# A 16 KiB copy from HBM to HBM as the first transfer of a streaming kernel

## The chip, the cores and the metric

The kernel runs on one core of one Trainium2 chip. The metric is the device time of one execution in microseconds, as a median over runs. A profile is one more execution, recorded by the hardware profiler; its span runs from the first to the last recorded instruction and is a little shorter than the device time.

## What is computed

The reference adds a scaled tensor to another. All tensors are bf16; `x` and `fx` have 512 x 32 x 640 elements (20.97 MB each), `alpha` is one number.

```python
B, S, D = 512, 32, 640
def reference(x, fx, alpha):
    return x + alpha * fx
```

So 41.94 MB have to be read from HBM and 20.97 MB written.

## The kernel before

Each tensor is seen as 128 rows (partitions) of 81,920 elements, that is 80 pieces of K = 1024 elements, or 160 KiB a row. `xv`, `fxv` and `ov` are these views of `x`, `fx` and the output. The tables `X` and `FX` cut the 80 pieces into tiles: x in three tiles of 32, 32 and 16 pieces, fx in five of 16, 16, 19, 16 and 13. The pool `wide` has two buffers for x tiles, `fs` two for fx tiles. The result is written over the x tile in SBUF (on-chip memory), and the x tile is what gets stored.

The order is written out by hand in `PLAN`, one step a line, and kept as it stands:

- `x i` (`load_x`, L73, its DMA at L77) loads x tile i. `X_CUTS` cuts tile 0 in two transfers: 4 pieces (1 MiB), then 28 pieces (7 MiB).
- `f j` (`load_f`, L82, DMA at L85) loads fx tile j.
- `a` (`alpha_to_lanes`, L109) loads alpha (DMA at L111), spreads it over 128 partitions with one matmul by a row of ones (L115), and copies the result from PSUM to `a_f` (L117).
- `c j i` (`compute`, L88, instruction at L92) does x + alpha * fx on VectorE (DVE) where fx tile j and x tile i overlap, one `scalar_tensor_tensor` instruction.
- `s i` (`store`, L102, DMA at L104) stores x tile i to the output.

All 13 DMA transfers are issued by SyncE (SP) on one queue, in the order of the plan: x tile 0 (two pieces), alpha, fx 0, fx 1, x 1, fx 2, store 0, fx 3, x 2, fx 4, store 1, store 2. The first six need no buffer that was used before and wait for nothing; the later ones wait for DVE or an earlier transfer to free a buffer or finish a tile. SP handles its instructions in order, so a waiting one holds up all that stand behind it.

At the end, `rest` (L126) makes SP wait for everything in `done` but the last store before the program's own closing wait for that store. `done` is the list to which each step appends its instruction.

The change adds one line between `store` and `lanes`, ahead of the loop over `PLAN`, and one constant.

Of the kernel before, what the change touches and what calls it, by code (L numbers as in the profile page):

```python
# [2 lines left out]

# [4 lines left out]

ACT = mybir.ActivationFunctionType
ALU = mybir.AluOpType  # L10
F32 = mybir.dt.float32
BF16 = mybir.dt.bfloat16

K = 1024
P = 128


X = [(0, 32), (32, 64), (64, 80)]
FX = [(0, 16), (16, 32), (32, 51), (51, 67), (67, 80)]

X_CUTS = {0: (4,)}
PLAN = """
x 0
a
f 0
f 1
x 1
c 0 0
f 2
c 1 0  # L30
s 0
f 3
x 2
c 2 1
f 4
c 3 1
c 3 2
s 1
c 4 2
s 2  # L40
"""


@with_exitstack
def kernel(
    ctx: ExitStack,
    tc: tile.TileContext,
    x: bass.AP,
    fx: bass.AP,
    alpha: bass.AP,  # L50
    out: bass.AP,
):

    nc = tc.nc
    xv = x.flatten_outer_dims().rearrange("(p n) d -> p (n d)", p=P)
    fxv = fx.flatten_outer_dims().rearrange("(p n) d -> p (n d)", p=P)  # L60
    ov = out.flatten_outer_dims().rearrange("(p n) d -> p (n d)", p=P)
    assert xv.shape[1] == X[-1][1] * K == FX[-1][1] * K

    consts = ctx.enter_context(tc.tile_pool(name="consts", bufs=1))
    psum = ctx.enter_context(tc.tile_pool(name="psum", bufs=1, space=bass.MemoryType.PSUM))
    wide = ctx.enter_context(tc.tile_pool(name="wide", bufs=2))
    fs = ctx.enter_context(tc.tile_pool(name="fs", bufs=2))
    ctx.enter_context(tc.manual_schedule())

    xt, ft = {}, {}  # L70
    done = []

    def load_x(i):  # L73
        a, b = X[i]
        xt[i] = wide.tile([P, max(e - s for s, e in X) * K], x.dtype, tag="x", name="x_t")
        for c, d in pairwise((a, *X_CUTS.get(i, ()), b)):
            r = nc.sync.dma_start(  # L77
                out=xt[i][:, (c - a) * K : (d - a) * K], in_=xv[:, c * K : d * K]
            )
            done.append(r)  # L80

    def load_f(j):  # L82
        a, b = FX[j]
        ft[j] = fs.tile([P, max(e - s for s, e in FX) * K], fx.dtype, tag="f", name="f_t")
        r = nc.sync.dma_start(out=ft[j][:, : (b - a) * K], in_=fxv[:, a * K : b * K])  # L85
        done.append(r)

    def compute(j, i):  # L88
        (fa, fb), (xa, xb) = FX[j], X[i]
        a, b = max(fa, xa), min(fb, xb)  # L90
        piece = xt[i][:, (a - xa) * K : (b - xa) * K]
        r = nc.vector.scalar_tensor_tensor(  # L92
            out=piece,
            in0=ft[j][:, (a - fa) * K : (b - fa) * K],
            scalar=lanes["a_f"][:],
            in1=piece,
            op0=ALU.mult,
            op1=ALU.add,
        )
        done.append(r)  # L100

    def store(i):  # L102
        a, b = X[i]
        r = nc.sync.dma_start(out=ov[:, a * K : b * K], in_=xt[i][:, : (b - a) * K])  # L104
        done.append(r)

    lanes = {}

    def alpha_to_lanes():  # L109
        a_1 = consts.tile([1, 1], alpha.dtype, name="a_1")  # L110
        done.append(nc.sync.dma_start(out=a_1[:], in_=alpha[None, :]))  # L111
        ones = consts.tile([1, P], alpha.dtype, name="ones")
        nc.vector.memset(ones[:], 1.0)  # L113
        a_ps = psum.tile([P, 1], F32, name="a_ps")
        done.append(nc.tensor.matmul(a_ps[:], ones[:], a_1[:], start=True, stop=True))  # L115
        lanes["a_f"] = consts.tile([P, 1], F32, name="a_f")
        nc.vector.tensor_copy(out=lanes["a_f"][:], in_=a_ps[:])  # L117

    does = {"x": load_x, "f": load_f, "c": compute, "s": store, "a": alpha_to_lanes}
    for step in PLAN.split("\n"):  # L120
        if step:
            what, *of = step.split()
            does[what](*map(int, of))


    rest = nc.sync.nop(nofuse=True)  # L126
    info = mybir.DependencyInfo(mybir.DependencyClass.Sync, mybir.DependencyReason.DATA)
    for i in done[:-1]:
        tc.add_manual_dep(rest.ins, i.ins.name, info, reason="all but the last store")


# [1 line left out]
_INS = ['x', 'fx', 'alpha']  # L133
_OUTS = [((512, 32, 640), 'bfloat16')]


# [23 lines left out]
```

## Time and profile before

| what | value |
|---|---|
| device time, median of 3 runs | 152.08 us (152.06 to 152.09) |
| span of the profiled execution | 150.2 us |
| DVE busy | 86.8 us, in 8 instructions |
| DMA | 1,730 packets, 62.92 MB, 419 GB/s over the span |
| HBM read, written | 41.94 MB, 20.97 MB |
| first piece of x (1024 KB), issue to landing | 4.8 us |
| second piece of x (7168 KB), issue to landing | 21.3 us |
| SP's first store and next load issued at | 66.78 and 67.19 us |

How to read the profile: an engine's busy time counts its compute instructions; issuing a DMA is not counted as busy. The row of the DMA queue tells how many packets went through it, their megabytes, and the time that they took as a share of what 16 DMA engines have in the span. The chain of waits follows the work that ended last back through what released it; the timeline lists instructions by their start; a table of windows gives, for each stretch of time, the busy time of each engine, the granted TensorE clock, and the DMA's share and rate. SPq is SP's queue of DMA issues. A window books a packet to the stretch in which it starts, so that short windows with long packets swing around the true rate.

The profiled execution's own time is its span of 150.2 us and what lies around the span; the difference to the median of the runs is 1.88 us.

### The profile page before, as it was taken

How to read it: one execution, taken by the hardware profiler on the slowest of the kernel's cores; microseconds unless marked ns; L12 is line 12 of the kernel's file. 1: busy time of each engine (PE TensorE's matmuls, PEld its weight loads, DVE VectorE, ACT ScalarE, POOL GpSimd, SP SyncE). 2: the span in 40 equal slices, each digit the busy share in tenths (PEclk: the TensorE clock that was granted, in tenths of full speed). 3: DMA queues.
4: the chain of work that ended last, by engine and by line, in shares of the span. 5: the costliest groups of instructions: out<-in, count | busy, mean ns of one | idle time of the engine just before them, and what ended most of it. 6: DMA issues, size and time to landing. Idle time of an engine off the chain costs nothing.

```text
span 150.2 us, 78 instructions
## 1 busy us (share of the span) xinstructions
PE 0.2 (0%) x1; PEld 0.1 (0%) x1; DVE 86.8 (58%) x8; POOL 0.2 (0%) x4
## 2 busy tenths in 40 slices
PE   0000000000000000000000000000000000000000
PEld 0000000000000000000000000000000000000000
DVE  0000000049999999970399999106999999980000
POOL 0000000000000000000000000000000000000000
DMA  5997989999969696999696999999999969696994
GB/s 179 589 428 305 489 384 419 436 454 471 576 297 559 279 559 279 497 394 435 279 559 279 559 401 410 445 419 419 419 393 454 620 279 559 279 559 297 454 463 183
DMA packets 1730, 62.92 MB, mean 419 GB/s; under 512 B 194, under 2 KB 194, under 8 KB 194
## 3 DMA queue, kind: packets, MB, share of 16 engines
q1 hardware_dynamic: 1730, 62.92, 98.1%
HBM read 41.94 MB, written 20.97 MB: 419 GB/s over the span
## 4 chain that ended last, share of the span: by engine, by line
DMA 54%; DVE 35%; SPq 1%; issue 0%; DVEq 0%
DMA f_t<-in_fx_dram 54%; DVE x_t L92 35%; SPq L77 1%; SPq L111 0%; DVEq L92 0%
## 5 line engine op out<-in xcount | busy, mean ns | idle before, releaser
L92 DVE SCALAR_TENSOR_TENSOR x_t<-f_t,a_f,x_t 128x16384 bf16<-128x16384 bf16 (+3 forms) x6 | 86.5, 14438 | 25.5 <-DMA f_t<-in_fx_dram 25.5
L117 DVE COPY a_f<-a_ps 128x1 f32<-128x1 f32 x1 | 0.2, 159 | 21.5 <-PE a_ps L115 21.5
L113 DVE MEMSET ones<- 1x128 bf16 x1 | 0.2, 165 | 0.8 <-PEq L144 0.8
L115 PE MATMUL a_ps<-a,ones 1*128 1x1 bf16 x1 | 0.2, 158 | 22.2 <-DMA a<-in_alpha_dram 22.2
L144 POOL MEMSET const-bfloat16-1.0<- 128x1 bf16 x1 | 0.1, 103 | 0.0
L144 POOL MEMSET const-uint8-127<- 128x1 uint8 x1 | 0.1, 103 | 0.0
L115 PEld LDWEIGHTS <-ones 1*128 1x128 bf16 x1 | 0.1, 100 | 1.0 <-DVE ones L113 1.0
L144 POOL MEMSET const-float32-1.0<- 128x1 f32 x1 | 0.1, 100 | 0.0
L144 POOL MEMSET const-float32-0.0<- 128x1 f32 x1 | 0.1, 99 | 0.2 <-issue 0.2
## 6 DMA issues: line engine op xcount, KB each, us to landing
f_t<-in_fx_dram SPq DMA_DIRECT2D x3, 4096.0 KB, 35.6
x_t<-in_x_dram SPq DMA_DIRECT2D x1, 7168.0 KB, 21.3
f_t<-in_fx_dram SPq DMA_DIRECT2D x1, 4864.0 KB, 24.1
x_t<-in_x_dram SPq DMA_DIRECT2D x1, 4096.0 KB, 19.2
out_dram<-x_t SPq DMA_DIRECT2D x1, 4096.0 KB, 14.9
f_t<-in_fx_dram SPq DMA_DIRECT2D x1, 3328.0 KB
x_t<-in_x_dram SPq DMA_DIRECT2D x1, 1024.0 KB, 4.8
out_dram<-x_t SPq DMA_DIRECT2D x2, 24.7
```

The lines of the kernel that those rows point to most:

```text
L77: r = nc.sync.dma_start(out=xt[i][:, (c - a) * K : (d - a) * K], in_=xv[:, c * K : d * K])
L92: r = nc.vector.scalar_tensor_tensor(out=piece, in0=ft[j][:, (a - fa) * K : (b - fa) * K], scalar=lanes["a_f"][:], in1=piece, op0=ALU.mult ...
L113: nc.vector.memset(ones[:], 1.0)
L115: done.append(nc.tensor.matmul(a_ps[:], ones[:], a_1[:], start=True, stop=True))
L117: nc.vector.tensor_copy(out=lanes["a_f"][:], in_=a_ps[:])
L144: nc = _bacc.Bacc("TRN2", target_bir_lowering=False, num_devices=1)
```

## The change

One more transfer is issued on SP's queue before the plan's first step. It copies the first 512 elements (1 KiB) of each of the first 16 rows of the view of x to the same place in the output, directly from HBM to HBM, 16 KiB in all. The first 512 elements of these rows belong to x tile 0, so store 0 writes the same bytes of the output again later, with the result. The transfer is appended to `done`. Nothing else differs; on all other engines the instructions stand as before, and on SP the others follow in their old order. In the changed file, lines from the new constant on move down by one, and those behind the new transfer by three.

```diff
 FX = [(0, 16), (16, 32), (32, 51), (51, 67), (67, 80)]
 
+HEAD = 16
 X_CUTS = {0: (4,)}
...
         r = nc.sync.dma_start(out=ov[:, a * K : b * K], in_=xt[i][:, : (b - a) * K])
         done.append(r)
 
+    done.append(nc.sync.dma_start(out=ov[:HEAD, :512], in_=xv[:HEAD, :512]))
+
     lanes = {}
```

## The prediction

> **What bounds the kernel now.** I read the page's busy times and DMA queue first, to see which resource is full, then the chain of waits and the timeline of the sync queue, then the DMA's rate in short windows at the two ends and wherever it sags.
>
> ```profile
> span 150.2 us, 78 instructions
> PE 0.2 (0%) x1; PEld 0.1 (0%) x1; DVE 86.8 (58%) x8; POOL 0.2 (0%) x4
> q1 hardware_dynamic: 1730, 62.92, 98.1%
> ```
>
> VectorE works 58% of the span; the one DMA queue works 98.1% of it, and 0.981 x 150.2 = 147.3 us. All 16 DMA engines together are the bound. Where are the 2.9 us in which they do nothing?
>
> ```profile
> 0.73 0.38 SPq L77
> 1.10 0.06 issue
> 1.16 0.42 SPq L77
> ```
>
> ```profile
> 1.63 0.32 SPq L111 DMA_DIRECT2D a<-in_alpha_dram  x1
> 1.99 0.87 SPq L85 DMA_DIRECT2D f_t<-in_fx_dram  x2
> 2.90 0.45 SPq L77 DMA_DIRECT2D x_t<-in_x_dram  x1
> ```
>
> The first fence is the chain of waits (start, duration, what), the second the timeline. SP issues the first piece of x at 0.73 us, and the next transfers start 0.43, 0.47 and 0.36 us after one another. The windows (length, busy times of PE, PEld, DVE, POOL, clock, DMA share, GB/s) say when data flows:
>
> ```profile
> 1.60:1.70 0.10, 0.00 (x0) 0.00 (x0) 0.00 (x0) 0.00 (x0) 1.00 0.00 0
> 1.70:1.75 0.05, 0.00 (x0) 0.00 (x0) 0.00 (x0) 0.00 (x0) 1.00 1.05 328
> 1.50:2.00 0.50, 0.00 (x0) 0.00 (x0) 0.00 (x0) 0.00 (x0) 1.00 1.13 246
> 2.00:2.50 0.50, 0.00 (x0) 0.00 (x0) 0.00 (x0) 0.00 (x0) 1.00 0.65 164
> 2.50:3.00 0.50, 0.00 (x0) 0.00 (x0) 0.00 (x0) 0.00 (x0) 1.00 0.86 311
> 3.00:3.50 0.50, 0.00 (x0) 0.00 (x0) 0.00 (x0) 0.00 (x0) 1.00 0.97 393
> 3.50:4.00 0.50, 0.00 (x0) 0.00 (x0) 0.00 (x0) 0.00 (x0) 1.00 0.98 410
> 4.00:4.50 0.50, 0.00 (x0) 0.00 (x0) 0.00 (x0) 0.00 (x0) 1.00 1.00 426
> ```
>
> Nothing moves before 1.70 us, 0.98 us after the first issue began (I put the start at 1.71). From there 147.3 us of transfer reach 149.0 us, and the last completion and closing barrier fill the rest. So the engines stand idle in front and behind only, and a delay of the first byte has no gap further on to vanish in. The rows also show a ramp: from 1.71 to 4.50 us, 2.79 us at the steady 426 GB/s would move 1,188 KB; the six half-microsecond rows add up to 975 KB. The missing 213 KB are 0.50 us of lost time.
>
> One more sag matters for a rival:
>
> ```profile
> 66.00:68.00 2.00, 0.00 (x0) 0.00 (x0) 0.76 (x1) 0.00 (x0) 1.00 1.35 584
> 68.00:70.00 2.00, 0.00 (x0) 0.00 (x0) 0.00 (x0) 0.00 (x0) 1.00 0.82 311
> 70.00:72.00 2.00, 0.00 (x0) 0.00 (x0) 0.00 (x0) 0.00 (x0) 1.00 1.26 311
> 72.00:74.00 2.00, 0.00 (x0) 0.00 (x0) 0.20 (x1) 0.00 (x0) 1.00 1.21 524
> ```
>
> A window books a packet where it starts, so a share can exceed 1. Each packet of fx here is one row of 38,912 bytes. At 66 to 68 us, 584 GB/s x 2 us are 30 packets, with 1.35 x 2 x 16 = 43.2 us of engine time: 1.44 us each. At 68 to 70 us there are 16 packets of 1.64 us, at 70 to 72 us 16 of 2.52 us. That is one per engine in each window, so every engine loses 0.20 + 1.08 = 1.28 us there. It comes 1 to 5 us after SP issued the first store, at 66.78 us.
>
> **The change, part by part.** Nothing is removed. One transfer is added ahead of everything on SP's queue; every later transfer keeps its place.
>
> *The issue.* The copy's issue takes the slot at 0.73 us, and the first x issue starts one step later. No row shows a 16-row copy from HBM to HBM. The nearest rows are steps from one issue's start to the next: 0.36 us for alpha (1 row) and 0.43 and 0.47 us for x (128 rows). Between 1 row and 128 rows, 16 rows give 0.36 + 15/127 x 0.07 = 0.37 us, which I take, since 16 lies close to 1; both ends, 0.36 and 0.47, go into the range. The first x byte then moves from 1.71 to 2.08 us. Five other issues are queued behind (x, alpha, fx twice, x) and all start 0.37 us later. That is covered: x's second piece keeps the engines busy until 21.3 us after its issue, by the page, thus to 22.5 us, and DVE, ready with alpha at 22.6 us, waits 9.7 us for fx anyway. Without that cover alpha's 0.37 us would be DVE's.
>
> *The data.* 16 KiB are 0.04 us at 426 GB/s, one KiB per engine if the rows are spread over all 16. It starts at 1.71 us and has the 0.37 us until x's descriptors are there. By size, the slow first packets bound it: in the row 1.50:2.00, 15 packets of 8 KiB took 1.13 x 0.5 x 16 = 9.0 us, 0.60 us each. A 1 KiB packet lies between 0.60/8 = 0.08 us (all by size) and 0.60 us (all latency). Up to 0.37 us it costs nothing; at 0.60 us it costs 0.23. I take nothing, as the lower end fits in the gap more than four times; without that gap it would cost 0.08.
>
> *The ramp.* If the copy takes over what makes the first packets slow, up to 0.50 us comes back; if not, 0. I take 0: x's descriptors reach all the engines together, as now, after the copy's bytes are gone.
>
> *Waits.* The first store writes the copy's bytes again and so must wait for it: it lands some 60 us before that store, where SP is waiting for DVE anyway. Without the order of these 60 us the store would stand still for the copy. The closing gather of all completions but the last store's gains the copy's, and is over 9.4 us before that store lands.
>
> *Other stages.* DVE's four waits end with fx's landing, so they and the later stores move with the stream: the second store is issued at 116.95 us, 3.5 us before the queue ahead of it runs out at 120.44 us, and both ends move alike.
>
> Sum against the profiled execution: 150.2 + 0.37 = 150.57 us span. The 1.88 us between that span and the median of 152.08 lie outside of it and do not change: 152.08 + 0.37 = 152.45 us.
>
> A rule speaks for a dearer copy. The Trainium skill, "DMA: Bandwidth & Descriptors", section "Anatomy of one DMA — SWDGE (gpsimd) path", gives a transfer a fixed cost of about 2.0 us, mostly the receipt for the write, and HBM as the slowest target. If that stood in series here, an estimate from that page would be 152.08 + 2.0 = 154.1 us. The queue's row speaks against series: 13 transfers run through this queue and only 2.9 us of the span are left without data, where 13 times 2.0 us would leave 26. By the row the sum stays at 152.45.
>
> **The rivals.**
>
> *A: the ramp shortens.* For it: 0.50 us of ramp, in which the engines are just starting. Against it: the copy ends before x starts, and its 16 KiB reach few of x's rows. All of it regained gives 152.45 - 0.50 = 151.95 us, half of it 152.20: no change that can be told.
>
> *B: the sag at 68 to 72 us is a cost of the first write to HBM, and the copy takes it at the start.* This one ends on the other side. For it: the sag falls just behind the first store's issue, hits all engines, and does not return with the later stores; the copy also writes HBM. Against it: the slowed packets are fx's reads, ahead of the store's own, and a single sag can have another cause. If all 1.28 us go and cost nothing in front: 152.45 - 1.28 = 151.17 us. If they are only moved to the front, 0.37 us of them hide in the gap and 0.91 are paid there: 152.08. It decides from 0.67 us of net saving on (the 0.37 of the issue and 0.30 for the bound below).
>
> *C: the copy holds up x's first bytes.* For it: both its ends are HBM, which no row prices. Against: 1 KiB per engine. Taking the 1.28 us sag as the price of a first write, less 0.37 us of gap, with the sag at 68 us still there: 152.45 + 0.91 = 153.36 us. It counts from a copy that occupies an engine over 0.37 us.
>
> That the copy is not first is no rival: in the built kernel's order for SP it stands ahead of all others, and it waits for no data.
>
> **How the numbers follow.** 0.2%, 0.30 us, is about what a measurement of this kernel can tell from no change, so "same" is 151.78 to 152.38. The plain shift gets 0.48 (0.44 slower, 0.04 same, at the shortest issue with a little ramp regained), A 0.21 (0.14 same, 0.07 faster when nearly all the ramp goes along with a cheap issue), B 0.20 (0.18 faster, 0.02 same), C 0.11 (slower). Slower: 0.44 + 0.11 = 0.55; same: 0.04 + 0.14 + 0.02 = 0.20; faster: 0.07 + 0.18 = 0.25. The likeliest case alone runs from 152.08 + 0.30 = 152.38 (shortest issue, a little ramp) to 152.08 + 0.47 + 0.23 = 152.78. The range for 8 in 10 goes down to B's full saving, 151.15, and up to 152.80; it leaves out most of C and little else.
>
> **What would show it.** Right: SP's first x issue near 1.10 us instead of 0.73; the first 8 KiB packets at about 2.08 us; the same deficit of some 0.5 us up to 4.9 us; fx's third load landing at 74.1 instead of 73.71 us; the sag of 1.28 us after the first store's issue; the span at 150.6. A: x's first piece landing less than 0.3 us later than its 5.5 us. B: no long packets at 68 to 72 us. C: the first x bytes later than 2.2 us. The forecast is wrong if the stream's start moves by other than 0.3 to 0.7 us, or if the time from first byte to last changes by over 0.2 us.

## The result, and the profile after

The changed kernel takes 152.91 us (median of 4 runs, 152.85 to 153.29) against 152.07 us for the kernel before in the same session: ratio 1.0061, 95% interval 1.0049 to 1.0072. It is slower, as forecast, but by 0.84 us where 0.37 were expected, and 0.11 us above the end of the range.

The page of the changed kernel, with the two rows that answer to those shown of before:

```profile
span 151.1 us, 80 instructions
...
q1 hardware_dynamic: 1762, 62.93, 97.4%
```

0.974 x 151.1 = 147.2 us of transfer, as before (147.3). The transfers have not become slower; the span has grown by 0.9 us without data. The chain of waits of the changed kernel (start, duration, what; L108 is the copy, L78 the loads of x) shows where:

```profile
0.73 0.61 SPq L108
1.33 0.06 issue
1.39 0.56 SPq L78
1.95 0.04 issue
1.99 0.43 SPq L78
...
50.57 24.05 DMA f_t<-in_fx_dram
```

The copy's issue keeps SP for 0.61 us, and the first x issue behind it takes 0.56 us where it took 0.38. So x's issue ends at 1.95 instead of 1.10 us. The last row shows the shift alive much later: fx's third load lands at 50.57 + 24.05 = 74.62, 0.91 us after its 73.71 of before.

Windows of the changed kernel at the start (length, busy times of PE, PEld, DVE, POOL, clock, DMA share, GB/s), from two tables:

```profile
2.10:2.40 0.30, 0.00 (x0) 0.00 (x0) 0.00 (x0) 0.00 (x0) 1.00 0.19 55
2.40:2.55 0.15, 0.00 (x0) 0.00 (x0) 0.00 (x0) 0.00 (x0) 1.00 0.00 0
2.55:2.60 0.05, 0.00 (x0) 0.00 (x0) 0.00 (x0) 0.00 (x0) 1.00 2.73 492
...
2.50:3.00 0.50, 0.00 (x0) 0.00 (x0) 0.00 (x0) 0.00 (x0) 1.00 1.27 246
3.00:3.50 0.50, 0.00 (x0) 0.00 (x0) 0.00 (x0) 0.00 (x0) 1.00 0.67 213
3.50:4.00 0.50, 0.00 (x0) 0.00 (x0) 0.00 (x0) 0.00 (x0) 1.00 0.83 311
4.00:4.50 0.50, 0.00 (x0) 0.00 (x0) 0.00 (x0) 0.00 (x0) 1.00 1.05 426
4.50:5.00 0.50, 0.00 (x0) 0.00 (x0) 0.00 (x0) 0.00 (x0) 1.00 1.01 426
```

The first row is the copy: 55 GB/s x 0.3 us = 16 KiB, in 0.19 x 0.3 x 16 = 0.91 us of engine time over 16 packets: at most 0.06 us each, as 16 packets of a few bytes are counted in. Then the engines wait, and x's first packets start at 2.57 us, 0.84 us later than before. The ramp is what it was: from 2.57 to 5.00 us, 426 GB/s would move 1,035 KB; the five rows add up to 811 KB; the missing 224 KB are 0.53 us (0.50 before).

The sag of before, in windows of the changed kernel that each hold one packet of every engine:

```profile
69.70:71.10 1.40, 0.00 (x0) 0.00 (x0) 0.00 (x0) 0.00 (x0) 1.00 1.05 445
71.10:72.60 1.50, 0.00 (x0) 0.00 (x0) 0.00 (x0) 0.00 (x0) 1.00 1.65 415
```

445 x 1.4 and 415 x 1.5 are 623 KB each, 16 packets of 38,912 bytes: 1.05 x 1.4 = 1.47 us and 1.65 x 1.5 = 2.48 us a packet, where 1.44 is normal. The sag is still there, 1.07 us an engine.

### The profile page after: what moved, and what is told of

Same layout as the page of the kernel before. It is cut to its first block, busy times and chain, and to the rows that moved or that the text cites. A ratio compares the mean times of both kernels' runs of the same rounds, so it can differ in the third digit from the quotient of the medians.

```text
span 151.1 us, 80 instructions
## 1 busy us (share of the span) xinstructions
PE 0.2 (0%) x1; PEld 0.1 (0%) x1; DVE 86.8 (57%) x8; POOL 0.2 (0%) x4
## 4 chain that ended last, share of the span: by engine, by line
DMA 53%; DVE 34%; SPq 1%; issue 0%; DVEq 0%
DMA f_t<-in_fx_dram 53%; DVE x_t L93 34%; SPq L78 1%; SPq L108 0%; SPq L114 0%; DVEq L93 0%
```

## The experiments

Three theories stood against one another. *Theory 1*: the loss is SP's issue, which is long when both ends of a transfer lie in HBM, and it counts because it stands ahead of the first byte. *Theory 2*: any transfer ahead of the first x load costs the same, or the cost belongs to a first use. *Theory 3*: the copy's data or write holds up the DMA engines. Each kernel ran beside runs of the kernel before, whose median was 151.91 to 151.99 us; ratios are to those.

| kernel | issue of the extra transfer, us | issue behind it, us | x's first byte, us | ratio (95%) |
|---|---|---|---|---|
| before | none | x 0.38 (it is first) | 1.73 | 1 |
| changed kernel | 0.61 | x 0.56 | 2.57 | 1.0061 (1.0049 to 1.0072) |
| load into SBUF, first | 0.38 | x 0.41 | 2.19 | 1.0037 (1.0024 to 1.0049) |
| copy to a scratch tensor, first | 0.58 | x 0.55 | 2.58 | 1.0050 (1.0037 to 1.0063) |
| copy with 128 rows, first | 0.64 | x 0.57 | 2.65 | 1.0068 (1.0046 to 1.0091) |
| two copies, first | 0.60, 0.57 | x 0.58 | 3.22 | 1.0092 (1.0079 to 1.0105) |
| copy on ScalarE's queue | 0.57 | its own queue | 1.74 | 1.0004 (0.9995 to 1.0013) |
| copy after six loads | 0.60 | none near | 1.73 | 1.0004 (0.9995 to 1.0013) |
| copy third | 0.61 | alpha 0.47 | 1.75 | 1.0004 (0.9995 to 1.0013) |
| copy second | 0.60 | x 0.57 | 1.73 | 1.0067 (1.0055 to 1.0080) |
| load into SBUF, second | 0.42 | x 0.41 | 1.75 | 1.0000 (0.9990 to 1.0010) |
| copy second, first piece doubled | 0.60 | x 0.58 | 1.75 | 0.9995 (0.9986 to 1.0004) |

Issue times are from the timeline, first bytes from windows of the trace.

### A load into SBUF in the copy's place

```diff
-    done.append(nc.sync.dma_start(out=ov[:HEAD, :512], in_=xv[:HEAD, :512]))
+    warm = consts.tile([HEAD, 512], x.dtype, name="warm")
+    done.append(nc.sync.dma_start(out=warm[:], in_=xv[:HEAD, :512]))
```

> The first transfer is again 16 rows of 1 KiB from x, but into a small tile in SBUF instead of the output in HBM. Theory 1 (SP's issue of a transfer with both ends in HBM is itself long, 0.61 us in the changed kernel, and lengthens the x issue behind it from 0.38 to 0.56 us): here the issue takes 0.32 to 0.38 us, the x issue behind it about 0.38, x's first byte moves by about 0.40 us from 1.73, and the time is 152.07 + 0.40 = 152.47 us. Theory 2 (anything placed ahead of the first x load costs what the change cost): 152.9 us. Theory 3 (the 16 rows, not the ends, make the issue long): issue 0.6 us, 152.9 us.

152.48 us (151.91 before). Its chain of waits:

```profile
0.72 0.38 SPq L109
1.10 0.06 issue
1.16 0.41 SPq L78
```

The same rows and bytes, with the target in SBUF, are issued in 0.38 us, and x's issue stays near its old length. Theory 2 in its first form (any transfer there costs the same) and the 16 rows as a cause fall. The cost, 0.57 us between the medians (0.36 to 0.74 by the interval), holds the expected 0.40 but lies above it; the first byte moved by 0.46.

### The copy after the six loads

```diff
 f 1
 x 1
+h
...
+    def head():
+        done.append(nc.sync.dma_start(out=ov[:HEAD, :512], in_=xv[:HEAD, :512]))
...
+    does = {..., "a": alpha_to_lanes, "h": head}
```

> The same copy, but issued after the six loads of the start instead of ahead of them. Theory 1 (the loss is the issue ahead of the first byte): the stream starts at 1.73 us as in the kernel before, the queue holds 60 us of work, and the copy costs its 16 KiB, 0.04 us: 152.07 to 152.15 us; its issue still takes 0.6 us where both ends in HBM make it long, and about 0.33 where the long issue belongs to the first place on the queue. Theory 3 (the copy's data or its write holds up the engines wherever it stands): 152.5 to 152.9 us.

151.96 us (151.91). The timeline row of its copy:

```profile
3.60 0.60 SPq L110 DMA_DIRECT2D out_dram<-in_x_dram  x1
```

The issue is as long when it stands seventh, so the length is not that of the first place. Behind 60 us of queued work it costs nothing that can be told. Theory 3 falls for a copy in mid-stream.

### The copy on ScalarE's queue

```diff
-    done.append(nc.sync.dma_start(out=ov[:HEAD, :512], in_=xv[:HEAD, :512]))
+    done.append(nc.scalar.dma_start(out=ov[:HEAD, :512], in_=xv[:HEAD, :512]))
```

> The same copy, issued from ScalarE's queue while SP issues the first piece of x. Theory 1 in its narrow form (the time is SP's own issue): SP's first issue is at 0.73 us and takes 0.38, x's first byte comes at 1.73 us, 152.07 to 152.15 us. If the two queues share what makes an issue long, SP's first issue takes 0.5 to 0.9 us and the time is 152.2 to 152.7 us. Theory 3 (the copy's data holds up the engines): 152.5 us or more.

152.01 us (151.91). Its timeline:

```profile
0.73 0.86 SPq L78 DMA_DIRECT2D x_t<-in_x_dram  x2
0.74 0.57 ACTq L108 DMA_DIRECT2D out_dram<-in_x_dram  x1
```

Both queues issue at the same moment and neither lengthens SP's x issue (0.86 us for two x issues, as before). The long issue holds up only the queue that issues it. The copy's data move early in the stream as well, between the first and the second piece of x (4.7 to 5.3 us). The same copy costs nothing that can be told once SP does not issue it.

### Two copies

```diff
     done.append(nc.sync.dma_start(out=ov[:HEAD, :512], in_=xv[:HEAD, :512]))
+    done.append(nc.sync.dma_start(out=ov[HEAD : 2 * HEAD, :512], in_=xv[HEAD : 2 * HEAD, :512]))
```

> Two copies of 16 rows of 1 KiB from x to the output (rows 0 to 15, then 16 to 31) ahead of the first load. Theory 1 (every issue of a transfer from HBM to HBM takes 0.60 us, and the x issue behind one is 0.19 us longer): the second copy adds 0.60 + 0.06 us, x's first byte goes from 1.73 to about 3.23 us, 1.50 us over the kernel before, and 0.19 more if the second copy's issue is lengthened too. Theory 2 (a cost of the first use, paid once): the second copy costs 0.37 to 0.43, 1.25 us over the kernel before. Theory 3 (engines held by the copy's data): no statement on the issue; the copies' packets would run up to x's first byte.

153.40 us (151.99): 1.41 more, against 0.84 for one copy. Its chain of waits:

```profile
0.72 0.60 SPq L108
1.33 0.06 issue
1.39 0.57 SPq L109
1.95 0.04 issue
2.00 0.58 SPq L78
```

The second copy's issue is about as long as the first's (0.57 and 0.60 us) and moves x's first byte by another 0.65 us, so the long issue is not a cost of the first use. It is not lengthened by the first; the x issue behind it is (0.58), and that lengthening is paid once.

### 128 rows, and a scratch tensor

```diff
-HEAD = 16
+HEAD = 128
```

> The copy has 128 rows of 1 KiB instead of 16. If the issue's 0.60 us grow with the rows (0.28 us over alpha's 0.32 for 16 rows, 0.018 a row), it takes 2.6 us and the time is some 2.8 us over the kernel before. If the issue costs the same for any count of rows, as for loads into SBUF (0.38 us with 16 rows and with 128), it takes 0.60 to 0.65, the first x byte comes at 2.57 us and the 128 KiB, 0.31 us at 426 GB/s, fit between the copy's first byte at 2.11 and that: 0.85 us over the kernel before.

```diff
-    done.append(nc.sync.dma_start(out=ov[:HEAD, :512], in_=xv[:HEAD, :512]))
+    scr = nc.dram_tensor("scr", (HEAD, 512), x.dtype, kind="Internal").ap()
+    done.append(nc.sync.dma_start(out=scr, in_=xv[:HEAD, :512]))
```

> The copy of 16 rows of 1 KiB goes to a scratch tensor in HBM that nothing else uses, again as the first transfer. Theory 1 (both ends in HBM make the issue long, whichever tensor): issue 0.60 us, the x issue behind it 0.57, x's first byte at 2.57, 0.7 to 0.95 us over the kernel before. If the long issue is the output tensor's (its first use, or the wait that the first store gains for the copy): issue 0.38, 0.4 to 0.5 us over.

152.92 us (151.99) and 152.73 us (151.97). The copy's row from the chain of waits, first with 128 rows and then into the scratch tensor:

```profile
0.73 0.64 SPq L108
```

```profile
0.73 0.58 SPq L109
```

Eight times the rows add 0.03 us to the issue, and a copy into a tensor that no store waits for is issued almost as slowly as one into the output. By the medians the two kernels lose 0.93 and 0.76 us, about what their first bytes lose. What is common to all the long issues is that both ends lie in HBM: most loads and stores, with one end in SBUF, took 0.33 to 0.43 us in these kernels (single ones in the burst of the start up to 0.69). The rows were 1 KiB long in every copy; whether their length counts was not tried.

The profile with 128 rows is of the slowest of that kernel's six executions (154.02 us; the others took 152.69 to 153.09). In it one engine starts its last data packet after 149.5 us, when none of the others has started one since 149.0: one engine fell behind here too, and that single execution does not say why. The copy's last packets run until 2.91 us in it, past x's first byte at 2.65, so that the 128 KiB did not fit ahead of x as expected.

### The copy second, and why that was dear

```diff
         for c, d in pairwise((a, *X_CUTS.get(i, ()), b)):
...
             done.append(r)
+            if c == 0:
+                done.append(nc.sync.dma_start(out=ov[:HEAD, :512], in_=xv[:HEAD, :512]))
```

> The same copy as second transfer, behind the first piece of x and ahead of the second. Theory 1: x's first byte stays at 1.73 us, the first piece keeps the engines busy to 4.9 us, the second piece's descriptors are there long before: 152.07 to 152.15 us. Theory 3 (its data holds up the engines): between 0.2 and 0.8 us over the kernel before, 152.3 to 152.9 us. If the x issue behind the copy is 0.19 us longer again, the lengthening belongs to whatever follows the copy; if not, to the first x load.

152.94 us (151.91): a miss for theory 1. x's first byte came at 1.73 us, and yet 1.03 us were lost. Windows of this kernel near the second piece of x, and at its end:

```profile
5.60:5.70 0.10, 0.00 (x0) 0.00 (x0) 0.00 (x0) 0.00 (x0) 1.00 1.71 573
...
148.00:149.00 1.00, 0.00 (x0) 0.00 (x0) 0.00 (x0) 0.00 (x0) 1.00 0.16 66
```

573 GB/s x 0.1 us are one packet of 57,344 bytes, the first of the second piece on one engine. It starts last of all, at 5.62 us, when every other engine has been at that piece since 5.38 at the latest, and takes 1.71 x 0.1 x 16 = 2.74 us, where such packets take 2.12. A second engine's first packet, at 4.98 us, took 3.25. At the end, 66 GB/s are two packets of 32 KiB that start after 148 us, when every other engine has started its last (in the kernel before no data packet starts after 148 us). They end at 149.7 and 150.0 us, the last of the others at 149.1: two engines finish alone. Here the slowest engine, and not the mean, sets the end.

Three kernels were made to find what held the two engines:

```diff
             if c == 0:
+                warm = consts.tile([HEAD, 512], x.dtype, name="warm")
+                done.append(nc.sync.dma_start(out=warm[:], in_=xv[:HEAD, :512]))
```

> The load of 16 rows of 1 KiB into a small SBUF tile stands second, between the two pieces of x, where the copy from HBM to HBM cost 1.0 us though x's first byte came at 1.73 us as before: there two of the 16 engines lost 1.1 and 0.6 us at the second piece of x and stayed behind to the end. If that is due to the copy's two HBM ends, this kernel takes 0.0 to 0.15 us over the kernel before and no engine falls behind. If any small transfer between the two pieces does it, 0.6 to 1.0 us over.

```diff
 x 0
+h
 a
```

> The copy stands third, behind both pieces of x and ahead of alpha. Its issue takes 0.60 us and alpha's behind it 0.45 to 0.5 instead of 0.32, while the queue holds 8 MiB of work: 0.0 to 0.15 us over the kernel before, if the 1.0 us of the copy in second place comes from standing where the engines are in their first 5 us. If a copy from HBM to HBM holds up some engines wherever it stands among large loads of the start, two engines fall behind at fx's first load by 0.5 to 1.1 us: 0.6 to 1.1 us over.

```diff
-X_CUTS = {0: (4,)}
+X_CUTS = {0: (8,)}
...
+            if c == 0:
+                done.append(nc.sync.dma_start(out=ov[:HEAD, :512], in_=xv[:HEAD, :512]))
```

> The copy in second place again, but with the first piece of x twice as long (8 of 32 pieces, 2 MiB), so that the engines come to the copy and the second piece of x at about 7.5 us instead of 4.9, while the second piece is issued at 1.80 us as before. If the 1.0 us of the copy in second place comes from the second piece reaching some engines late, the 2.5 us of margin take it away: 0.0 to 0.2 us over the kernel before, no engine behind. If some engines are held up by the copy itself whenever the second piece follows it, 0.6 to 1.1 us over.

152.01 us (151.99), 152.03 us (151.97) and 151.97 us (151.99): none of the three costs anything that can be told. The timeline of the copy in third place, its copy and the alpha issue behind it, 0.47 instead of 0.32 us:

```profile
1.63 0.61 SPq L110 DMA_DIRECT2D out_dram<-in_x_dram  x1
2.29 0.47 SPq L116 DMA_DIRECT2D a<-in_alpha_dram  x1
```

With the first piece doubled, the copy's issue and the one behind it are as long as in second place (0.60 and 0.58 us), the second piece's packets are a little smaller (49,152 bytes), and the 1.0 us is gone.

The place of the copy's data alone is not the cause. These are its rows in the table of DMA issues (KB, us from issue to landing), from ScalarE's queue and then as SP's second transfer:

```profile
out_dram<-in_x_dram ACTq DMA_DIRECT2D x1, 16.0 KB, 5.1
...
out_dram<-in_x_dram SPq DMA_DIRECT2D x1, 16.0 KB, 4.6
```

Both land at 5.8 us (0.74 + 5.1 and 1.16 + 4.6), and in both traces the packets run from 4.7 to 5.3 or 5.4 us, between the two pieces of x; yet the first costs nothing that can be told. What differs is when SP is through with the issue of x's second piece: at 1.59 us with the copy on ScalarE's queue, at 2.05 with the load second, at 2.37 with the copy second. The first engine comes to that piece at 4.7 to 4.9 us (at 7.2 with the first piece doubled). So the loss goes with the shortest time between the issue and the need, 2.3 us against about 2.9 or more. No kernel made it that short without a copy in front on the same queue, so whether the copy itself counts beyond the time that its issue takes is not separated. That the piece's descriptors reach two engines late is a reading that fits; it was not shown.

### The sag at 70 us

Rival B of the prediction had put the sag down to the first write to HBM. The changed kernel, and the two kernels that copy after the six loads and in third place, write HBM earlier and keep it (1.07, 0.9 and 1.0 us an engine). Two more kernels, without the copy, asked whether it belongs to the first store.

```diff
 c 0 0
+t
 f 2
...
+    def tiny():
+        done.append(nc.sync.dma_start(out=ov[:16, :512], in_=xt[0][:16, :512]))
```

> No copy; in its stead the first 512 elements of 16 rows of the result are stored a first time right after the first VectorE instruction, at 49.6 us (the first store writes them again). It asks what the sag in the third fx load (1.3 us an engine, 3 to 5 us behind the first store's issue at 66.8 us) belongs to. If to the first transfer from SBUF to HBM: the sag comes at 53 to 62 us and not at 70; the time stays within 0.15 us of the kernel before, or falls by up to 1.2 us if a small store pays less. If to the place in the stream or to the large store: the sag stays at 70 to 73 us and the time within 0.15 us.

```diff
 c 0 0
 f 2
+t
 c 1 0
-s 0
+u
...
+    def half(a, b):
+        done.append(nc.sync.dma_start(out=ov[:, a * K : b * K], in_=xt[0][:, a * K : b * K]))
...
+    "t": lambda: half(0, 16), "u": lambda: half(16, 32)
```

> No copy; the first store is cut in two halves, the first issued at 50 us right after the third fx load, the second at 66.8 us as before; the data keep their order in the queue. If the sag in the third fx load belongs to the issue of the first large store, it moves to about 53 us; if to the place in the stream or to the issues at 67 us, it stays at 70 to 73 us. The time stays within 0.2 us of the kernel before either way.

152.14 us (151.99; ratio 1.0009, 1.0000 to 1.0017) and 151.97 us (151.97; ratio 1.0002, 0.9993 to 1.0011). Windows of the second, with half of the store issued at 50 us:

```profile
52.00:54.00 2.00, 0.00 (x0) 0.00 (x0) 2.00 (x1) 0.00 (x0) 1.00 1.21 524
...
70.00:72.00 2.00, 0.00 (x0) 0.00 (x0) 0.00 (x0) 0.00 (x0) 1.00 1.19 311
```

At 52 to 54 us, 32 packets of 32 KiB take their normal 1.21 us each; at 70 to 72 us, 16 packets of fx take 1.19 x 2 = 2.38 us instead of 1.44. The sag stays where it was. So it does with the small early store, whose packets run at 60.4 to 61.0 us, ahead of the third fx load: at 70 to 72 us 16 packets of fx take 2.34 us there. Neither the first write, nor the first read of SBUF by a store, nor the issue of the first large store is its cause. The data of the first large store follow right behind the third fx load in every kernel here, and no run moved them away. The sag may belong to them, to the place in the stream or to the issues near 67 us; that stays open.

## Why the prediction was half right

- *The bound.* Right. The DMA's transfer time is unchanged (147.2 against 147.3 us), and each kernel with an extra transfer ahead of x lost what its first byte lost, to within 0.11 us. x's first byte comes a steady 0.62 to 0.66 us after the end of its own issue (1.73 - 1.10 before, 2.57 - 1.95 changed, 3.22 - 2.58 with two copies).
- *The issue.* This is the step that failed, a term that was mis-sized: "Between 1 row and 128 rows, 16 rows give 0.36 + 15/127 x 0.07 = 0.37 us". The step from the copy's issue to x's is 0.66 us, 0.29 more. The interpolation went by rows, along which an issue's length hardly changes (0.38 us for 16 rows into SBUF, 0.61 and 0.64 us for copies of 16 and 128 rows). What counts was not varied in any row of before: all its transfers have one end in SBUF. The two ends of the bound, 0.36 and 0.47, came from the same kind of transfer and so bounded nothing.
- *The issue behind.* The text moved the following issues without lengthening them ("all start 0.37 us later"). An x issue behind a copy takes 0.55 to 0.58 us instead of 0.38 to 0.42, in six kernels. This adds 0.18 us in the changed kernel and was not in the sum at all: the term was put at nothing without a reason. 0.37 + 0.29 + 0.18 = 0.84 us, the measured shift of the first byte and the difference of the medians. The profile of before had a small case of it: the fx load that SP issues right behind the first store, at 67.19 us, takes 0.42 us, and those at 49.59 and 94.31, with no issue just ahead of them, 0.33.
- *The data and the write.* Right for the first place: at most 0.06 us a packet, done 0.2 us before x's first. The Trainium skill, "DMA: Bandwidth & Descriptors", section "Anatomy of one DMA — SWDGE (gpsimd) path", gives about 2.0 us for a transfer's fixed part and calls descriptor generation small. The copy does land 2.0 us after its issue began. But this latency was not in series with the stream; what cost here was SP's issue, 0.61 us, and the longer issue behind it. The section's figures are for the GpSimd path, and the measured issue decides here.
- *The waits.* The first store's wait for the copy cost nothing: the scratch tensor, on which no store waits, is no faster beyond the intervals.
- *Rival A* (a shorter ramp) did not happen: 0.53 us against 0.50. *Rival B* did not happen: 1.07 us of sag remain. *Rival C* gave first x bytes later than 2.2 us as its sign, and they came at 2.57; but its cause was absent: the copy's packets were gone by 2.40 us, and x's first byte came as long after the end of its issue as before. The direction, slower, was forecast for the right reason, the time of one more issue; the size was not.

No version here beats the kernel before beyond its interval.

## What to carry to other kernels

A stream that is DMA-bound from end to end turns each delay of its first byte into run time, so what stands ahead of the first load is priced by the issue time of the queue, not by its bytes (16 and 128 KiB cost nearly the same here). Price an issue by a row with the same two ends, and count what it does to the issue behind it; where no such row exists, the bound must be wider than the spread of the other kind. A transfer that has to be issued early and is needed late belongs behind the first large loads or on another engine's queue, where it cost nothing here.

## What was not expected of the hardware

- A copy from HBM to HBM takes 0.57 to 0.64 us to issue on SP or ScalarE, with 16 or 128 rows of 1 KiB, against 0.33 to 0.43 us for most loads and stores; an issue of x or alpha right behind it takes 0.15 to 0.20 us longer.
- With the same copy issued by SP between the first and second piece of x, two of 16 engines fell behind at the second piece, for good (packets 0.6 and 1.1 us longer): 1.03 us of run time with the first byte on time. With 2.5 us more of margin, or with the copy on ScalarE's queue, nothing was lost.
- On the mean an engine loses 0.7 to 1.3 us at about 70 us in every profile taken, at the end of the third fx load, wherever the first store was issued.
